# Softmax attention beside a feature-map attention on one core: part of the first score maxima computed from score differences

## The chip, the cores and the metric

The kernel runs on one core of a Trainium2 chip. The core has five engines that run at the same time, each with its own in-order queue of instructions: TensorE (PE, matrix products into PSUM), VectorE (DVE), ScalarE (ACT), GpSimd (POOL) and SyncE (SP, which here only issues DMAs). PSUM has eight banks of 128 partitions by 512 fp32 columns. The metric is the device time of one execution in microseconds (us), the median over several runs.

## The reference

Two attention layers stand side by side, and their outputs are concatenated along the features. Sequence length is 2048, model width 512, 32 heads of 16 features; inputs are bf16.

```python
# A: softmax attention
qkv = (x @ wqkv) -> q, k, v           # each [32 heads, 2048, 16]
scores = einsum("bhqd,bhkd->bhqk", q, k) * 16 ** -0.5
p = softmax(scores, axis=-1)
a = einsum("bhqk,bhkd->bhqd", p, v) -> [2048, 512] @ wo
# B: linear attention with a softmax feature map
pq, pk = q @ w_phi, k @ w_phi          # per head, 16 x 16
phi = concat([softmax(p), softmax(-p)])
kv, z = phi_k^T v, sum_s phi_k
b = (phi_q kv) / (phi_q z + 1e-6) -> [2048, 512] @ wo
out = concatenate([a, b], axis=-1)
```

Layer A has 32 x 2048 x 2048 scores, and every one of them is computed twice: once to find each row's maximum, once to take the exponential. Layer B is small and runs beside it.

## The kernel before, in words

**Tiling of layer A.** The heads are packed in 8 groups `g` of four heads, one head in each quarter of 32 partitions (`QT`, `KT`: [128, 8, 2048], queries and keys with features on partitions). Two groups share one projection: a matrix product of 128 output columns gives eight heads, of which the even four belong to one group and the odd four to the other. `proj_kq` makes one such chunk of 512 positions: four PE matmuls, then for the very first chunk ("direct") two ACT passes that mask the bank into the two groups, and for all others a staging copy by ACT into `SG` (line 553) and two POOL passes that mask it (lines 557 and 561). The keys carry ones in the unused feature rows, so that the queries can carry the negated row maximum there.

**Units.** The work is cut in units of a group and a stretch of queries: first four units of 128 queries (group 0, queries 0 to 511), then units of 256, at the end units of 128 again. Each unit passes through:

1. *Maxima* (`try_m1`, `try_m1_of`): for every 128 queries, each of the four heads (`r`, a row quarter of PE) and each of the four key chunks `kc` of 512, one matmul writes a bank of 128 queries by 512 scores (line 944). DVE reduces two banks at a time to two columns of `part` (line 952). A full unit has its columns reduced once more to the row maximum (`row_max`, line 974). For the first four units and the last ones the maximum goes into the queries by two short DVE operations (lines 985, 986), a PE transposition (line 988) and a DVE addition (line 991); for the others by POOL and two DMAs.
2. *Exponentials* (`try_m2`): the scores are computed again, transposed, with the maximum already subtracted by the extra rows (line 1034), and ACT takes `exp(0.25 s)` from a bank into a slot of the ring `pT` (28 slots).
3. *Values* (`try_pv`, line 1100): PE multiplies the slots with `VP`, the values with a column of ones, which gives the sums too; then the division, and the output projection.

**Layer B** runs in 32 steps (`fm`), the first released at 40 us and then one every 29.5 us. Its buffers `pB`, `uB` and `oB` are not used before that.

**What sets the order.** The order of all instructions is written out beforehand by a planner in the kernel's own code: a simulation with fixed durations per instruction. Each engine takes, whenever it is free, the ready instruction of the lowest `prio`; PE decides by the backlogs of DVE and ACT whether it feeds the maxima or the exponentials next, and fits in projections ("jobs", each with a due number `want`) and dummy matmuls (lines 1336 and 1351) where they do not hurt. `job_late` gives the price that a waiting job may put on the scores; before 60 us it is so high that any ready job goes ahead. Some two dozen weights of these decisions are drawn anew for every 36 us of the plan from a list of numbers, `SEEDS0`. The resulting order is fixed in the program, with semaphores between the engines.

**The start.** The first 512 rows of x come by plain loads into `SG` and are transposed by PE (`turn_x(0, t)`), the next 512 by one load into an unused slice of `QT` and by PE as well; rows 1024 to 2047 come by DMA transposes straight into `xAT` (line 496), in four pieces for each 512 rows. The weights of the first projections are loaded in two small pieces, the rest in three large ones behind the first transposes.

Of the kernel before, what the change touches and what calls it, by code (L numbers as in the profile page):

```python
# [7 lines left out]
ALU = mybir.AluOpType  # L8
# [172 lines left out]
def bass_concat_heads__softmax_full_mha__linear_kernel_hedgehog__prompt_kernel(  # L181
# [8 lines left out]
    NKT = 16  # L190
    NC = 4
    RING = 28
    SEG = 36
    SEEDS0 = [484, 2, 930, 619226, 78, 78407, 78375275, 78375663478, 78375275210, 78375275322, 78375275348780669,
              337514, 422, 709462, 422743, 709830676, 422280059592, 422280059592983, 1365, 680, 874585, 933,
              704, 134, 317297294, 227, 219559, 961, 141970821483, 219559543039, 154753, 268, 80, 80802]
    VB = 7

    BW = 18
# [8 lines left out]
    for c in range(NC):  # L208
        for g in range(NG):
# [3 lines left out]
            for q0, nq in cuts:  # L213
                units.append((g, c, 512 * c + q0, nq))
    NU = len(units)

    with contextlib.ExitStack() as es:
        block = es.enter_context(nc.Block())
# [265 lines left out]
        for t in range(4):  # L484
# [5 lines left out]
        dma("xn4", lambda e: e.dma_start(  # L490
            QT[:, 5, :].rearrange("p (t n) -> p t n", n=512),
            A_x[0][512:1024, :].rearrange("(t p) n -> p t n", p=128)), (), [("Q", 5, k) for k in range(NC)], prio=0.1,
            us=0.5, land=5.8)
        for c in range(2, NC):
            for ct in range(4):
                dma("xa%d" % c, lambda e, ct=ct, c=c: e.dma_start_transpose(
                    xAT[:, ct, c * 512:(c + 1) * 512], A_x[0][c * 512:(c + 1) * 512, ct * 128:(ct + 1) * 128]), (),
                    [("xA", c, ct)], prio=0.3 if c == 2 else 0.7, us=1.29, land=5.0)
# [24 lines left out]
        def proj_kq(kind, G, c, want, direct):  # L523
            col = (0 if kind == "q" else 512) + 128 * G
            T = QT if kind == "q" else KT
            K = "Q" if kind == "q" else "K"
            sl = slice(c * 512, (c + 1) * 512)
            j = job(quads(lambda e, b, ct: e.matmul(  # L528
                PS[:, b, :], wA[:, ct, col:col + 128], xAT[:, ct, sl], start=(ct == 0), stop=(ct == 3))),
                want, [("wA", 0 if kind == "q" else 1) + ((0,) if G == 0 else ())] + [("xA", c, t) for t in range(4)])  # L530
            projs.append(j.node)
            if kind == "k":
                kv_projs.append(j.node)
            if direct:
                n = []
                for gl in range(2):
                    g = 2 * G + gl
                    if kind == "q":
                        n.append(act(
                            lambda g=g: T[:, g, sl], lambda: PS[:, j.bank, :], ACT.Copy, 512, ["kmask"],  # L540
                            [(K, g, c)], n[:1], prio=1, scale=kmask[:, gl:gl + 1]))
                    else:
                        n.append(act(
                            lambda g=g: T[:, g, sl], lambda: PS[:, j.bank, :], ACT.Identity, 512,
                            ["kmask", "kone"], [(K, g, c)], n[:1], prio=1 + 0.5 * gl, scale=kmask[:, gl:gl + 1],
                            bias=kone[:, 1 - gl:2 - gl]))
                    kq_nodes[(kind, g, c)] = n[-1]
                    n[-1].deps.append(j.node)
                n[-1].frees = ("G", j)
                return  # L550
            k = stg[0] % 4
            stg[0] += 1
            evac(j, act(lambda: SG[:, k, :], lambda: PS[:, j.bank, :], ACT.Copy, 512, (), [("SG", k)], prio=2))
            for gl in range(2):
                g = 2 * G + gl
                if kind == "q":
                    kq_nodes[(kind, g, c)] = pool(lambda e, g=g, gl=gl: e.tensor_scalar(
                        T[:, g, sl], SG[:, k, :], kmask[:, gl:gl + 1], kmask[:, gl:gl + 1], ALU.mult, ALU.mult), 0.8,
                        [("SG", k), "kmask"], [(K, g, c)], prio=1)
                else:  # L560
                    kq_nodes[(kind, g, c)] = pool(lambda e, g=g, gl=gl: e.tensor_scalar(  # L561
                        T[:, g, sl], SG[:, k, :], kmask[:, gl:gl + 1], kone[:, 1 - gl:2 - gl], ALU.mult, ALU.add),
                        0.72, [("SG", k), "kmask", "kone"], [(K, g, c)], prio=1)
# [22 lines left out]
            return [kq_nodes[("q", g, c, a)] for a, b_ in QCUT if a < q0 + nq and b_ > q0]  # L586

        QCUT = ((0, 128), (128, 512))

        def proj_v(kt, want):  # L590
            j = job(quads(lambda e, b, ct: e.matmul(  # L591
                PS[:, b, :], xAT[:, ct, kt * 128:(kt + 1) * 128], wA[:, ct, 1024:1536],
                start=(ct == 0), stop=(ct == 3))), want, [("wA", 2)] + (
                    [("xA", kt // 4, kt % 4)] if kt < 8 else [("xA", kt // 4, ct) for ct in range(4)]))
            projs.append(j.node)
            kv_projs.append(j.node)
            v_nodes[kt] = evac(j, act(
                lambda: VP[:, kt, :, 0:16], lambda: PS[:, j.bank, :].rearrange("p (h d) -> p h d", d=16), ACT.Copy,
                512, (), [("V", kt)], prio=2))

        def turn_x(c, t):
            src = (lambda: SG[:, t, :]) if c == 0 else (lambda: QT[:, 4 + c, 512 * t:512 * t + 512])
            j = job(quads(lambda e, b, ct: e.matmul(
                PS[:, b, ct * 128:(ct + 1) * 128], src()[:, ct * 128:(ct + 1) * 128], ident[:],
                start=(ct == 0), stop=True, skip_group_check=True)), (-10 if c == 0 else 1.5) + 0.1 * t, ["ident"] + (
                    [("SG", t)] if c == 0 else [("Q", 4 + c, k) for k in range(NC)]), cols=128)
            projs.append(j.node)
            s0 = 512 * c + 128 * t
            keys = [("xA", c, t)]
            if t % 2 and c == 0:  # L610
                n = dve(lambda e: e.tensor_copy(
                    xAT[:, :, s0:s0 + 128], PS[:, j.bank, :].rearrange("p (a b) -> p a b", b=128)), 512, (), keys, prio=0)
# [8 lines left out]
        proj_kq("k", 0, 0, 0, True)  # L621
        for a, b_ in QCUT:
            first_q(a, b_, -0.5 if a == 0 else 1)
        for c in range(1, NC):
            if c == 1:
                for t in range(4):
                    turn_x(c, t)
            proj_kq("k", 0, c, 2 * c, False)
# [275 lines left out]
        def try_m1(single):  # L904
            u0 = m1["u"]
            for u in range(u0, 4 if u0 < 4 else min(u0 + 1, NU)):
                if u not in m1_of:
                    m1_of[u] = {"m": 0, "left": [], "half": None}
                if m1_of[u]["m"] < units[u][3] // 8 and try_m1_of(u, m1_of[u], single):
                    return True  # L910
            return False

        def try_m1_of(u, sm, single):
# [36 lines left out]
            off = p_off(u)  # L950
            deps = [n] + [rm_nodes[v] for v in range(u - 4, u - 1) if v in rm_nodes and v % 2 == ub]
            d = dve(lambda e: e.tensor_reduce(  # L952
                part[:, ub, off + m:off + m + k], PS[:, banks[0]:banks[-1] + 1, :],
# [6 lines left out]
            if sm["m"] == nq // 128 * 16:  # L960
# [3 lines left out]
            return True  # L964

        def p_off(u):
            return 16 * (u // 2) if u < 4 else 0
# [1 line left out]
        def row_max(u):  # L969
# [3 lines left out]
            off = p_off(u)  # L973
            rm_nodes[u] = dve(lambda e: e.tensor_reduce(  # L974
                mrow[:, ub, 0:4 * nt].rearrange("p (r q) -> p r q", r=4),
                part[:, ub, off:off + 16 * nt].rearrange(
                    "p (q k r) -> p r q k", r=4, q=nt), AX.X, ALU.max), 16 * nt + 40, (),
                [("mrow", ub)], r1_nodes[u], prio=0)
            mv = mrow[:, ub, 0:4 * nt]
# [386 lines left out]
        def try_pe():  # L1366
# [20 lines left out]
            for e in (("dve", "act") if d <= a + K.DA else ("act", "dve")):  # L1387
                if e == "dve" and d < K.TM and try_m1(d < K.DS):
                    return True
                if e == "act" and a < K.TA and slots_ready() and try_m2():  # L1390
                    return True
            if d >= K.TM:
# [258 lines left out]
```

## Time and profile before

| | |
|---|---|
| median of 3 runs | 1216.81 us (1216.23 to 1217.08) |
| the profiled execution | 1216.89 us |
| its span, first to last instruction | 1215.2 us |
| busy: PE, DVE, ACT, POOL | 1191.8, 1179.7, 1162.4, 841.5 us |
| granted TensorE clock | 1.000 |

How to read the lines that follow: L952 is line 952 of the kernel; an instruction is named by its engine, its operation and what it writes from what, for instance `part<-PS` for a reduction from PSUM into the tile `part`. Many ACT instructions carry line 398 and many DVE copies line 402 or 611, since one helper records them; they are told apart by their tiles. In a row of groups, the first number behind the bar is the time in which at least one instruction of the group ran, the second the mean length in ns of one; behind the second bar stands the idle time of the engine in front of them and what ended it. One instruction's bar is longer than its step, because the next one begins before it has drained. In a row of a timeline the first number is the start, the second the length of a run of equal instructions, and the bracket the idle time before. In the chain of waits a row is a stretch of the chain that ended last. In a table by stage the columns are: stretch, length, busy us and count of each engine, granted clock, share of DMA, GB/s.

### The profile page before, as it was taken

What the parts mean: (1) busy time and instruction counts of PE and PEld (TensorE: products, weight loads), DVE (VectorE), ACT (ScalarE), POOL (GpSimd) and SP (SyncE); (2) the same over time, 40 slices, a digit from 0 to 9 for tenths busy, and PEclk for the clock granted to TensorE, in tenths of its full rate; (3) what the DMA queues carried; (4) which work ended last, traced back from release to release, by engine and by line L of the source; (5) the groups of instructions that cost most, each with busy time, mean ns of one, the idle gap of its engine ahead of it and who ended that gap; (6) DMA issues with size and microseconds to landing.
All of it is one profiled execution on the core that took longest, in us unless ns stands there. A gap on an engine that the chain in (4) does not pass through costs nothing.

```text
span 1215.2 us, 39617 instructions
## 1 busy us (share of the span) xinstructions
PE 1191.8 (98%) x16953; PEld 574.2 (47%) x16953; DVE 1179.7 (97%) x1124; ACT 1162.4 (96%) x2364; POOL 841.5 (69%) x1194
## 2 busy tenths in 40 slices
PE   8999999999999999999999999999999999999998
PEld 4443444444444444544444444444444444545565
DVE  6999999999999999999999999999999999999993
ACT  4889999999999999999999999999999999999998
POOL 5498888776766766778898888888889894311120
PEclk9999999999999999999999999999999999999999
DMA  8200010001000100011112112111111111000000
GB/s 200 46 6 6 9 24 9 9 6 26 9 11 21 25 7 9 14 27 18 21 29 42 39 24 34 31 29 21 27 26 28 30 35 25 17 10 9 10 11 22
DMA packets 100209, 30.49 MB, mean 25 GB/s; under 512 B 87488, under 2 KB 100032, under 8 KB 100032
## 3 DMA queue, kind: packets, MB, share of 16 engines
q1 hardware_dynamic: 99072, 27.49, 11.4%
q8 instruction: 133, 2.18, 0.7%
q10 hardware_dynamic: 960, 0.46, 0.1%
q14 instruction: 44, 0.36, 0.1%
HBM read 4.21 MB, written 4.19 MB: 7 GB/s over the span
## 4 chain that ended last, share of the span: by engine, by line
ACT 37%; DVE 34%; PE 28%; DMA 0%; issue 0%; ACTq 0%; DVEq 0%
DVE part L952 34%; ACT pT L398 33%; PE PS L1034 9%; PE PS L944 5%; PE PS L1336 4%; PE PS L1100 4%; PE PS L825 1%; ACT eB L398 1%; PE PS L1351 1%; PE PS L684 1%; PE PS L591 1%; PE PS L528 1%; PE PS L761 1%; ACT X L398 1%; ACT xAT L398 1%; DMA wA<-in_A_wqkv_dram 0%
## 5 line engine op out<-in xcount | busy, mean ns | idle before, releaser
L952 DVE TENSOR_REDUCE part<-PS 128x2 f32<-128x1024 f32 x1024 | 1168.9, 1209 | 9.3 <-PE PS L944 5.2
L398 ACT ACTIVATE pT<-PS 128x512 bf16<-128x512 f32 x2034 | 1051.4, 690 | 20.5 <-PE PS L1034 11.5
L1034 PE MATMUL PS<-QT,KT 32*128 32x256 bf16 (+1 forms) x4480 | 700.2, 263 | 7.3 <-ACT pT L398 1.3
L1336 PE MATMUL PS<-zmv,ones_t 32*128 32x256 bf16 x3753 | 602.8, 271 | 0.3
L944 PE MATMUL PS<-KT,QT 32*128 32x512 bf16 x2570 | 482.2, 382 | 6.5 <-DVE part L952 4.1
L1034 PEld LDWEIGHTS PS<-QT,KT 32*128 32x128 bf16 x4480 | 242.3, 92 | 269.5 <-ACT pT L398 182.5
L1336 PEld LDWEIGHTS PS<-zmv,ones_t 32*128 32x128 bf16 x3753 | 284.7, 92 | 33.5 <-ACT X L398 3.7
L1100 PE MATMUL PS<-pT,VP 128*17 128x256 bf16 (+1 forms) x4480 | 195.6, 266 | 2.1 <-ACT pT L398 0.7
L944 PEld LDWEIGHTS PS<-KT,QT 32*128 32x128 bf16 x2570 | 124.6, 91 | 128.3 <-DVE part L952 64.5
L1161 POOL TENSOR_TENSOR lr<-lr,cons 128x8 f32<-128x8 f32 (+1 forms) x66 | 104.7, 1587 | 55.1 <-DMA lr<-X 55.1
L1100 PEld LDWEIGHTS PS<-pT,VP 128*17 128x17 bf16 x4480 | 68.5, 88 | 98.9 <-issue 83.4
L804 POOL TENSOR_TENSOR den_t<-den_t,cons 128x32 f32<-128x32 f32 x16 | 87.2, 5451 | 0.5
L711 POOL TENSOR_SCALAR sB<-sB 128x256 f32<-128x256 f32 (+2 forms) x96 | 68.8, 716 | 6.6
L747 POOL TENSOR_TENSOR wA<-eB,rB 128x1024 bf16<-128x1024 bf16 x32 | 61.7, 1927 | 14.8 <-ACT rB L398 14.6
L1171 POOL TENSOR_TENSOR QT<-X,Yd 128x256 bf16<-128x256 f32 (+1 forms) x66 | 45.7, 692 | 36.7 <-DMA Yd<-Yd 36.6
L724 POOL TENSOR_TENSOR sB<-eB 128x512 f32<-128x512 bf16 x32 | 36.9, 1153 | 45.4 <-ACT eB L398 45.4
L998 POOL TENSOR_SCALAR stage<-mrow 128x8 bf16<-128x8 f32 (+1 forms) x64 | 15.4, 240 | 75.4 <-DVE mrow L974 75.2
L709 POOL TENSOR_TENSOR sB<-uB 128x256 f32<-128x256 f32 (+2 forms) x96 | 45.7, 476 | 5.8
L698 POOL TENSOR_TENSOR sB<-pB 128x256 f32<-128x256 f32 x32 | 23.1, 721 | 32.8 <-ACT pB L398 32.3
L1351 PE MATMUL PS<-zmv,ones_t 128*32 128x512 bf16 x464 | 42.0, 386 | 0.2 <-ACT X L398 0.2
L561 POOL TENSOR_SCALAR KT<-SG,kmask,kone 128x512 bf16<-128x512 bf16 x30 | 22.7, 768 | 27.1 <-ACT SG L398 27.1
L713 POOL TENSOR_TENSOR uB<-sB,uB 128x256 f32<-128x256 f32 x64 | 37.8, 591 | 3.8
(118 smaller groups left out, 817.5 us busy)
## 6 DMA issues: line engine op xcount, KB each, us to landing
Yd<-Yd SPq DMA_DIRECT2D x232, 16.0 KB, 2.2
out_dram<-xAT SPq DMA_DIRECT2D x16, 128.0 KB, 1.7
out_dram<-OA SPq DMA_DIRECT2D x15, 128.0 KB, 1.7
QT<-mcols SPq DMA_DIRECT2D x116, 2.0 KB
mcols<-stage SPq DMA_TRANSPOSE x64, 2.3
lr<-X SPq DMA_DIRECT2D x58, 4.0 KB
Yd<-lr SPq DMA_DIRECT2D x58, 4.0 KB
wA<-in_A_wqkv_dram SPq DMA_DIRECT2D x2, 384.0 KB, 4.8
```

Of the source, the lines that this page charges most:

```text
L398: n = mk("act", lambda ds: P.op("act", lambda e: e.activation(out_(), in_(), func, **kw), ds), reads, writes, deps, occ=c + (0.093 if sbuf ...
L709: pool(lambda e, w=w, rw=rw: e.tensor_tensor(rw, t3[:, :, 0:w], t3[:, :, w:2 * w], ALU.subtract), us, tb, ["sB"])
L711: pool(lambda e, w=w: e.tensor_scalar(sB[:, 0:64 * w], sB[:, 0:64 * w], 1.0, 0.0, ALU.mult, ALU.max), us1, ["sB"], ["sB"])
L747: pool(lambda e: e.tensor_tensor(phiB[k].rearrange("p (g f) -> p g f", f=16), e3, rB[:, i, :].unsqueeze(2).broadcast_to([128, 64, 16]), AL ...
L804: pool(lambda e: e.tensor_tensor(den_t[:, :], den_t[:, :], cons[:, 0:32], ALU.pow), 5.42, ["cons"], ["den"])
L944: fns = [lambda e, rr=rows[i], b=banks[i]: e.matmul(PS[:, b, :], QT[32 * rr:32 * rr + 32, g, q0 + 128 * qt:q0 + 128 * qt + 128], KT[32 * r ...
L952: d = dve(lambda e: e.tensor_reduce(part[:, ub, off + m:off + m + k], PS[:, banks[0]:banks[-1] + 1, :], AX.X, ALU.max), 512 * k, (), (), d ...
L1034: fns = [lambda e, kt=kg * ns + j, j=j: e.matmul(PS[:, bank, j * nq:(j + 1) * nq], KT[32 * r:32 * r + 32, g, kt * 128:(kt + 1) * 128], QT[ ...
L1100: fns.append(lambda e, r=r, s=s, kt=kt, j=j: e.matmul(PS[32 * r:32 * r + 17, VB, 0:nq], VP[:, kt, 8 * (g // 2) + 2 * r + g % 2, :], pT[:, ...
L1161: pool(lambda e: e.tensor_tensor(lr[:, ub, 0:nr], lr[:, ub, 0:nr], cons[:, 0:nr], ALU.pow), 0.17 * nr + 0.2, ["cons"], [("lr", ub)], prio=2)
L1336: n = pe_op([lambda e, r=r: e.matmul(PS[:, VB, 0:FW], ones_t[32 * r:32 * r + 32, :], zmv[32 * r:32 * r + 32, 0:FW], tile_position=(32 * r, ...
L1351: pe_op([lambda e, q=q: e.matmul(PS[32 * q:32 * q + 32, VB, :], ones_t[:, 0:32], zmv[:, :], tile_position=(0, 32 * q), **kw) for q in rang ...
```

## The change

Four things change.

1. *Maxima from differences.* For the first four units (group 0, 128 queries each), `DIFF` marks pairs of key chunks: the pair of chunks 2 and 3 in all four units and the pair of chunks 0 and 1 in units 2 and 3, which is six groups of four heads, 24 pairs of banks. For such a pair, PE computes the difference of the two banks (queries times chunk kc+1, plus the negated queries in `oB` times chunk kc, into one bank), ACT takes its ReLU into one of four fp32 buffers (`uB` and `pB` of layer B), PE computes the bank of chunk kc, and one DVE instruction adds the two and reduces the sum with a maximum: max(a, b) = a + relu(b - a). A group of pairs may begin only before 36 us (`DT`); one that has not begun then goes the old way. POOL makes the negated queries.
2. *x rows 1024 to 1535* are loaded plainly into a slice of `QT` and transposed by PE (`turn_x(2, t)`), as rows 512 to 1023 were already. The DMA transposes of the last 512 rows get the rank of the earlier ones.
3. *First K projection*, chunks 1 to 3: the even group's half is masked by ACT straight from PSUM (`direct == 2`), the odd half goes through `SG` and POOL as before.
4. *The planner*: the high price of a late job holds until 18 us (`JT`) and not until 60 us, the due numbers of two chunks move, and all the numbers in `SEEDS0` are others.

```diff
+    DT = 36
+    KM = 2
+    JT = 18
...
+    DIFF = "01,01,11,11".split(",")
...
-        dma("xn4", lambda e: e.dma_start(
...
-        for c in range(2, NC):
+        for c in (1, 2):
+            dma("xn%d" % (4 * c), lambda e, c=c: e.dma_start(
+                QT[:, 4 + c, :].rearrange("p (t n) -> p t n", n=512),
+                A_x[0][512 * c:512 * c + 512, :].rearrange("(t p) n -> p t n", p=128)), (),
+                [("Q", 4 + c, k) for k in range(NC)], prio=0.1, us=0.5, land=5.8)
+        for c in range(3, NC):
             for ct in range(4):
                 dma("xa%d" % c, lambda e, ct=ct, c=c: e.dma_start_transpose(
...
-                for gl in range(2):
+                for gl in range(1 if direct == 2 else 2):
...
+        def neg_q():
+            for a, b_ in QCUT:
+                qn_nodes[a] = pool(lambda e, a=a, b_=b_: e.tensor_scalar(
+                    oB[:, a:b_], QT[:, 0, a:b_], -1.0, 1.0, ALU.mult, ALU.mult), 0.3 if a == 0 else 0.65, (), ["oB"],
+                    [kq_nodes[("q", 0, 0, a)]], prio=0)
...
+        RD = [(uB[:, 0:512], ("uB", 0)), (uB[:, 512:1024], ("uB", 1)), (pB[:, 0, :], ("pB", 0)),
+              (pB[:, 1, :], ("pB", 1))]
...
+        def try_diff():
...
+                fns = [lambda e, a=a, i=i: e.matmul(
+                    PS[:, b, :], a[32 * r:32 * r + 32, q0:q0 + 128],
+                    KT[32 * r:32 * r + 32, g, (kc + i) * 512:(kc + i + 1) * 512],
+                    start=(i == 1), stop=(i == 0), tile_position=(32 * r, 0)) for a, i in ((QT[:, g, :], 1), (oB, 0))]
+                n = pe_op(fns, need, "row", (r, r), (b,))
+                k = rd_free.pop(0)
+                buf, key = RD[k]
+                x = act(lambda: buf, lambda: PS[:, b, :], ACT.Relu, 512, (), [key], [n], prio=0.5)
...
+        def try_sum(u, sm):
...
+                n = pe_op(fns, [x], "row", (r,), (b,))
...
+                d = dve(lambda e: e.tensor_tensor_reduce(
+                    buf, PS[:, b, :], buf, 1.0, -3.0e38, ALU.add, ALU.max, part[:, u % 2, o:o + 1]), 530, (), [key],
+                    [n, x], prio=1)
...
+                if e == "act" and a < K.TA and m1["u"] < len(DIFF) and try_diff():
+                    return True
...
         def job_late(now):
-            if now < 60.0:
+            if now < JT:
                 return 9.0
```

More of the change, by code (lines that the diff above doesn't have):

```diff
@@ L907, in try_m1 @@
                 if u not in m1_of:
-                    m1_of[u] = {"m": 0, "left": [], "half": None}
-                if m1_of[u]["m"] < units[u][3] // 8 and try_m1_of(u, m1_of[u], single):
-                    return True
+                    m1_of[u] = {"m": 0, "left": [], "half": None, "p": 0, "dl": None, "al": []}
+                sm = m1_of[u]
+                if sm["m"] < units[u][3] // 8:
+                    if by_diff(u, sm["m"]):
+                        if try_sum(u, sm):
+                            return True
+                    elif try_m1_of(u, sm, single):
+                        return True
@@ new lines, in try_sum @@
+        def try_sum(u, sm):
+            now = state["now"]
+            g, c, q0, nq = units[u]
+            kc = sm["m"] // 4 % 4
+            if nfree() < 1 or held["m"] >= 4:
+                return False
+            for ent in sm["al"]:
+                r, k, x = ent
+                if x.start is None or not pe_ok("row", (r,)):
+                    continue
+                if x.done > now + 0.4:
+                    push(x.done - 0.4)
+                    continue
+                sm["al"].remove(ent)
+                b = take("m", 1)[0]
+                fns = [lambda e: e.matmul(
+                    PS[:, b, :], QT[32 * r:32 * r + 32, g, q0:q0 + 128],
+                    KT[32 * r:32 * r + 32, g, kc * 512:(kc + 1) * 512],
+                    start=True, stop=True, tile_position=(32 * r, 0))]
+                n = pe_op(fns, [x], "row", (r,), (b,))
+                buf, key = RD[k]
+                o = p_off(u) + sm["p"] + r
+                d = dve(lambda e: e.tensor_tensor_reduce(
+                    buf, PS[:, b, :], buf, 1.0, -3.0e38, ALU.add, ALU.max, part[:, u % 2, o:o + 1]), 530, (), [key],
+                    [n, x], prio=1)
+                d.frees = [("m", b)]
+                rd_free.append(k)
+                r1_nodes.setdefault(u, []).append(d)
+                last["m1"] = (fns, (r,), n, d)
+                if not sm["dl"] and not sm["al"]:
+                    sm["m"] += 8
+                    sm["p"] += 4
+                    sm["dl"] = None
+                    group_done(u, sm)
+                return True
@@ L975, in row_max @@
                 mrow[:, ub, 0:4 * nt].rearrange("p (r q) -> p r q", r=4),
-                part[:, ub, off:off + 16 * nt].rearrange(
+                part[:, ub, off:off + m1_of[u]["p"]].rearrange(
                     "p (q k r) -> p r q k", r=4, q=nt), AX.X, ALU.max), 16 * nt + 40, (),
```

77 lines of the change are left out of this document (59 added, 18 removed).

## The prediction

> **What bounds the kernel now.** I read the page's busy shares and slices first, then a table by stage, then the chain of waits, then the timelines of the first 60 us.
>
> ```profile
> span 1215.2 us, 39617 instructions
> PE 1191.8 (98%) x16953; PEld 574.2 (47%) x16953; DVE 1179.7 (97%) x1124; ACT 1162.4 (96%) x2364; POOL 841.5 (69%) x1194
> ...
> ACT 37%; DVE 34%; PE 28%; DMA 0%; issue 0%; ACTq 0%; DVEq 0%
> ```
>
> Three engines look full. PE's share is padded, because lines 1336 and 1351 are dummy matmuls; VectorE (DVE) and ScalarE (ACT) share the chain almost evenly. So it must be seen, stage by stage, which of the two has room:
>
> ```profile
> core 0: us, PE busy (x) PEld busy (x) DVE busy (x) ACT busy (x) POOL busy (x), PEclk, DMA share, GB/s
> 11.00:35.00 24.00, 23.03 (x166) 9.84 (x167) 20.35 (x21) 14.15 (x26) 8.10 (x13) 1.00 0.77 184
> 35.00:60.00 25.00, 24.10 (x282) 11.71 (x280) 24.89 (x33) 20.94 (x41) 10.74 (x15) 1.00 0.17 39
> 60.00:100.00 40.00, 37.81 (x552) 18.27 (x551) 39.64 (x38) 35.55 (x73) 36.65 (x57) 1.00 0.04 6
> 100.00:1100.00 1000.00, 989.00 (x13683) 463.30 (x13681) 997.74 (x928) 981.91 (x2008) 757.48 (x1043) 1.00 0.11 21
> 1100.00:1192.20 92.20, 91.12 (x1762) 54.22 (x1759) 91.44 (x93) 86.58 (x181) 18.81 (x39) 1.00 0.06 10
> 1192.20:1215.30 23.10, 18.40 (x458) 10.47 (x454) 3.63 (x11) 19.42 (x37) 0.00 (x0) 1.00 0.08 26
> ```
>
> DVE is idle for 2.26 + 0.76 = 3.0 us between 100 and 1192 us: from 100 us until its last score maximum (1192.2 us) it alone sets the pace. ACT is idle for 9.85 us in 11 to 35, 4.06 in 35 to 60 and 4.45 in 60 to 100: 18.4 us in all, for it waits there for the first maxima. From 100 to 1192 ACT shows 18.1 + 5.6 = 23.7 us of idle time in small pieces. After 1192.2 us ACT works off the exponentials that are left, and the run ends 23 us later:
>
> ```profile
> core 0: us, PE busy (x) PEld busy (x) ACT busy (x), PEclk, DMA share, GB/s
> ...
> 110.00:1180.00 1070.00, 182.20 (x3968) 61.25 (x3968) 982.57 (x1910) 1.00 0.11 21
> ...
> 1192.20:1216.00 23.80, 5.11 (x292) 4.04 (x288) 17.47 (x28) 1.00 0.08 25
> ```
>
> These are the instructions that touch the exponentials' tile pT: 28 ACT instructions, 17.5 us, come after the last maximum. So two clocks run one behind the other, DVE's and ACT's, and the end is ACT's. A gain on DVE is worth its full size only if ACT is earlier too.
>
> **The change, part by part.** The prices:
>
> ```profile
> L952 DVE TENSOR_REDUCE part<-PS 128x2 f32<-128x1024 f32 x1024 | 1168.9, 1209 | 9.3 <-PE PS L944 5.2 <-PE PS L1034 2.3 <-PE PS L1336 0.2
> L991 DVE TENSOR_TENSOR QT<-PS,QT 128x128 bf16<-128x128 f32 x6 | 1.7, 279 | 0.0
> L611 DVE CAST xAT<-PS 128x512 bf16<-128x512 f32 x2 | 1.3, 684 | 5.3 <-PE PS L603 5.3
> L402 DVE COPY X<-PS 128x128 f32<-128x128 f32 x2 | 0.6, 290 | 5.0 <-PE PS L1113 5.0
> ```
>
> ```profile
> 44.97 0.09 DVE mrow L974
> ...
> 93.08 18.10 DVE part L952 x16
> ...
> 590.66 10.78 ACT pT L398 x22
> ```
>
> *24 pairs.* Two banks cost one reduction; back to back that is 18.10/16 = 1.131 us. Now ACT takes ReLU(S1-S0) of one bank and DVE adds S0 and takes the maximum over one bank. The trace has no such instruction. From below: one pass over 512 columns cannot be under half of 1.131, 0.57. From above: if the second operand doubled the time, 1.13, nothing saved. Nearest rows: the two 512-column CASTs out of PSUM take 1.3 us together, each 0.684, so the second starts about 0.61 after the first; and a TENSOR_TENSOR with two inputs (279 ns for 128 columns) is no dearer than a COPY with one (290). I take 0.61. DVE saves 24 x (1.131 - 0.61) = 12.5 us, between 0 and 24 x 0.56 = 13.5. The Trainium skill, "VectorE: DVE Perf Modes", § Two Vector instructions with no wait between them, says that an op which also writes out its accumulator is two instructions, the main one and an accumulator read. No instruction of this trace writes an accumulator, so the trace cannot judge it. At the step of the shortest DVE row above (0.09) that would take 24 x 0.09 = 2.2 us off the saving, 10.3 in place of 12.5; I leave it out of the sum and keep it in the range.
>
> ACT pays 24 ReLUs over 128x512 from PSUM; its exponentials of that shape step at 10.78/22 = 0.49 us: 24 x 0.49 = 11.8 us.
>
> *The rest on ACT:*
>
> ```profile
> 12.23 0.81 ACT L398 ACTIVATE KT<-PS,kone,kmask 128x512 bf16<-128x512 f32 x1
> 12.26 0.40 PE L603 MATMUL PS<-ident,QT 128*128 128x128 bf16 x4
> 12.90 0.63 ACT L398 ACTIVATE xAT<-PS 128x512 bf16<-128x512 f32 x1
> ...
> 19.88 0.60 ACT L398 ACTIVATE VP<-PS 128x512 bf16<-128x512 f32 x1 [4.32 <-PE PS L591]
> ```
>
> Turning rows 1024 to 1535 on PE adds four jobs of four 128-column matmuls (0.40 us each, 1.6 in all, where PE runs dummies) and four ACT copies: 4 x 0.49 = 2.0 us. The even half of K, chunks 1 to 3, is a scaled and biased ACT pass straight from PSUM (0.67 us from its start at 12.23 to the next at 12.90): 3 x 0.67 = 2.0 us; the staging copy stays, for the odd half. ACT's added work is 11.8 + 2.0 + 2.0 = 15.8 us, against 18.4 us of idle time before 100 us. It fits, but little is left. If that cover were gone, all 15.8 us would be on ACT's clock.
>
> *Off the path:*
>
> ```profile
> 14.81 3.03 POOL L561 TENSOR_SCALAR KT<-SG,kmask,kone 128x512 bf16<-128x512 bf16 x4 [4.42 <-ACT SG L398]
> ...
> 2.73 5.54 SPq L496 DMA_TRANSPOSE xAT<-in_A_x_dram  x4
> ...
> 10.04 5.20 SPq L496 DMA_TRANSPOSE xAT<-in_A_x_dram  x4
> ...
> 1.73 5.67 DMA wA<-in_A_wqkv_dram
> ```
>
> POOL loses three K passes of 0.76 us and gains the negated Q (512 columns in two pieces, some 0.8 us by the same row); it works 8.1 of the 24 us, so that is free. SP issues one 512 KB load in place of four transposes (5.54 us); the transposes of the last chunk move from 10.04 to about 3.3, ahead of the big weight loads, which move from 8.3 (2.73 + 5.54) to some 8.8, and what stands behind them (Wo, the other branch's weights) goes out about 5 us sooner. The new load shares the DMA engines with the first K weights, which land at 7.40 (1.73 + 5.67) and start everything: at the 184 GB/s of the table's first row 512 KB are 2.8 us of transfer; with half of that in the way of the weights the start is 1.4 us later, and since 512 KB of transposes leave the same place, it may as well be 1.4 us sooner; I take 0, in the middle.
>
> *PE's jobs (JT 60 to 18) and DVE's waits:*
>
> ```profile
> 11.02 3.71 DVE L952 TENSOR_REDUCE part<-PS 128x2 f32<-128x1024 f32 x3 [2.41 <-PE PS L944]
> 15.29 4.79 DVE L952 TENSOR_REDUCE part<-PS 128x2 f32<-128x1024 f32 x4 [0.56 <-PE PS L944]
> 21.01 3.48 DVE L952 TENSOR_REDUCE part<-PS 128x2 f32<-128x1024 f32 x3 [0.94 <-PE PS L944]
> 25.32 3.49 DVE L952 TENSOR_REDUCE part<-PS 128x2 f32<-128x1024 f32 x3 [0.83 <-PE PS L944]
> ...
> 29.64 1.23 DVE L952 TENSOR_REDUCE part<-PS 128x2 f32<-128x1024 f32 x1 [0.32 <-PE PS L944]
> ...
> 34.03 2.36 DVE L952 TENSOR_REDUCE part<-PS 128x2 f32<-128x1024 f32 x2 [0.71 <-PE PS L1034]
> ...
> 27.44 1.83 PE PS L591 x8
> ```
>
> Behind its first reduction DVE waits 0.56 + 0.94 + 0.83 + 0.32 + 0.71 = 3.4 us, mostly for score matmuls that stand behind pairs of V projections (1.83 us, line 591, in the chain). From 18 us on such jobs now yield, and chunk 3 of x comes earlier: up to 3.4 us back. But the change adds a wait: DVE's in-order sum needs a ReLU, which needs a score difference, and behind a waiting sum stand the row maxima that release the exponentials. ACT must give DVE a ReLU (0.49) per 0.61 us while it also copies K, V and x. I take 0.5 us of the 3.4 as net gain, range -6 to +3.4.
>
> *New draws.* All 34 planner draws change, so the order of everything changes. DVE has 3.0 us to win in 100 to 1192, with no such bound on a loss; I take 0, range -4 to +3.
>
> **The sum.** DVE's clock: 12.5 + 0.5 = 13.0 us earlier at the last maximum. ACT's clock: 18.4 - 15.8 = 2.6 us earlier at 100 us if DVE's lead lets it run without gaps. The gap of 10.4 us must come from ACT's 23.7 us of small gaps in 100 to 1192 and from the tail, where no maxima compete. Nothing in the trace says how much of them DVE's larger lead can fill; I take half, 5.2: 2.6 + 5.2 = 7.8 us. Span 1215.2 - 7.8 = 1207.4. The profiled execution took 1216.89, 1.7 us more than its span: 1209.1. That execution is 0.1 us from the median of 1216.81, so I say 1209.
>
> **Rivals.**
> *ACT follows fully.* If all the small gaps can be used, the end moves with DVE: 1216.8 - 13 = 1204, and with all 3.4 us of the waits back 1201. For it: ACT is more idle than DVE in every stage. Against: a single exponential shows a longer bar than its step, so ACT's true room is uncertain, and gaps behind PE's job bursts do not go away with a larger lead.
> *ACT is the clock.* If the small gaps are PE's, only the head's 2.6 us remain: 1214.2; and if some of the six groups begin after 36 us, where the code goes back to plain reductions, each gives up 4 x 0.52 = 2.1 us of DVE's saving, so that little of the change takes place: 1214 to 1218. Against: ACT has 9.85 us idle in the very stretch where the groups run.
> *Slower: ReLUs arrive late.* Place: 15 to 45 us. DVE's price per pair is then not 0.61 but ACT's spacing of the ReLUs. One copy (0.49) between two ReLUs makes 0.98; at 1.13 the saving is gone; with two copies it is 1.47, and 24 x (1.47 - 1.13) = 8.1 us are lost while ACT's head is no earlier: 1225. It decides from 1.23 us per pair on (2.4 us lost). For it: 16 V, 4 x and several K copies fall into that stretch. Against: the ReLUs have a better rank (0.5) than V and staging copies (2). The same comes about if the sum itself runs at half rate: at 1.13 nothing is saved on DVE, the DVE clock loses its waits, and 1217 to 1220 follows. [...]
>
> **Chances.** About 0.2% (2.4 us) is what a measurement of this kernel can tell from no change. Forecast (1205 to 1213) 0.48; ACT follows fully 0.21; ACT the clock, or few groups run 0.14, nearly all within 0.2%; late ReLUs or a dear sum 0.17, slower. So faster 0.69, same 0.14, slower 0.17. The range is 1201 to 1219: it leaves out the slower case and a sliver below the fastest. The forecast's own range is 1205 to 1213.
>
> **What would show it.** The new DVE group: 24 instructions with a step near 0.61 (right) or 1.1 (half rate). The 24 ReLUs on ACT between 15 and 40 us. The last maximum near 1179 instead of 1192.2, and a longer tail behind it, 25 to 29 us instead of 23. ACT's idle time in 11 to 100 us under 6 instead of 18.4. DVE's waits behind the first reduction at 3 us or less. It is wrong if DVE idles before the sums for ACT, if the K weights land after 8.5 us, or if DVE's idle time in 100 to 1192 grows past 5 us.

## The result and the profile after

The changed kernel takes 1211.16 us (median of 6 runs, 1210.99 to 1212.92) against 1216.53 us before (6 runs, 1216.18 to 1217.08). The ratio is 0.996, 95% interval 0.9947 to 0.9972: 5.4 us faster, by medians. The profiled execution has a span of 1209.4 us, 5.8 less than before. The page's shares and chain come first:

```profile
span 1209.4 us, 39536 instructions
PE 1186.3 (98%) x16833; PEld 569.1 (47%) x16833; DVE 1173.3 (97%) x1195; ACT 1174.2 (97%) x2393; POOL 838.9 (69%) x1193
...
ACT 48%; PE 28%; DVE 22%; POOL 1%; issue 1%; DMA 0%; ACTq 0%; DVEq 0%; POOLq 0%
```

DVE's and ACT's busy times, 17 us apart before, are now 1 us apart, and of the chain that ended last ACT has 48% in place of 37, DVE 22% in place of 34. The table by stage has the cuts of the one before, except that the last maximum is now at 1187.0 us:

```profile
core 0: us, PE busy (x) PEld busy (x) DVE busy (x) ACT busy (x) POOL busy (x), PEclk, DMA share, GB/s
11.00:35.00 24.00, 22.46 (x159) 7.67 (x157) 22.69 (x57) 22.64 (x44) 8.07 (x16) 1.00 0.94 174
35.00:60.00 25.00, 24.29 (x272) 11.55 (x273) 24.43 (x35) 21.45 (x40) 3.82 (x8) 1.00 0.18 33
60.00:100.00 40.00, 39.46 (x574) 19.75 (x573) 39.52 (x39) 36.80 (x74) 28.49 (x46) 1.00 0.06 11
100.00:1100.00 1000.00, 987.30 (x13614) 462.58 (x13609) 995.52 (x965) 988.23 (x2024) 773.37 (x1065) 1.00 0.11 21
1100.00:1187.00 87.00, 85.79 (x1718) 50.45 (x1714) 86.24 (x90) 82.49 (x173) 17.37 (x35) 1.00 0.06 10
1187.00:1209.50 22.50, 18.72 (x444) 10.80 (x442) 2.95 (x10) 18.76 (x38) 0.00 (x0) 1.00 0.08 27
```

Both clocks can be read from this table and the one before, by adding the busy columns and taking the rest of each stage as idle.

**DVE, 11 us to the last maximum.** Busy 1174.1 before, 1168.4 now: 5.7 less. Idle 7.1 before, 7.6 now. Together 5.2 us, and the last maximum moved by 1192.2 - 1187.0 = 5.2.

**ACT, 11 us to the end.** Busy 1158.6 before, 1170.4 now: 11.8 more. Idle 45.8 before, 28.1 now: 17.6 less. Together 5.8 us, the change of the span. The idle time came from before 100 us (18.4 to 8.1) and from 100 us to the last maximum (23.7 to 16.3); behind that it is 3.7 in both.

The new instructions, and DVE's reductions, by groups (the numbers behind the bar are busy time and the mean length of one, and behind the second bar the idle time ahead):

```profile
L1058 DVE TENSOR_REDUCE part<-PS 128x2 f32<-128x1024 f32 x957 | 1095.4, 1213 | 7.6 <-PE PS L1050 3.8 <-PE PS L1144 1.2 <-PE PS L1446 0.9
L1058 DVE TENSOR_REDUCE part<-PS 128x1 f32<-128x512 f32 x86 | 54.4, 681 | 1.7 <-PE PS L1144 1.0 <-PE PS L1446 0.2
...
L1004 DVE CUSTOM_DVE_ANT_0 uB<-PS,uB 128x512 f32<-128x512 f32 x12 | 8.2, 686 | 0.1
L1004 DVE CUSTOM_DVE_ANT_0 pB<-PS,pB 128x512 f32<-128x512 f32 x12 | 8.2, 685 | 0.4 <-PE PS L997 0.2
L1004 DVE DVE_READ_ACCUMULATOR2_ANT part<- 128x1 f32 x24 | 2.0, 82 | 0.0
...
L406 DVE COPY pB<-PS 128x512 f32<-128x512 f32 x2 | 1.4, 686 | 0.0
...
L406 DVE COPY X<-PS 128x256 f32<-128x256 f32 x2 | 0.8, 420 | 0.0
...
L406 DVE CAST vB<-PS 128x512 bf16<-128x512 f32 x1 | 0.7, 683 | 0.0
```

All 24 pairs took the new way, and DVE waited 0.1 + 0.4 = 0.5 us in all ahead of the sums. The timeline gives the step of a sum:

```profile
10.99 3.71 DVE L1058 TENSOR_REDUCE part<-PS 128x2 f32<-128x1024 f32 x3 [2.41 <-PE PS L1050]
15.40 6.01 DVE L1058 TENSOR_REDUCE part<-PS 128x2 f32<-128x1024 f32 x5 [0.70 <-PE PS L1050]
21.33 0.68 DVE L1004 CUSTOM_DVE_ANT_0 uB<-PS,uB 128x512 f32<-128x512 f32 x1
21.94 0.08 DVE L1004 DVE_READ_ACCUMULATOR2_ANT part<- 128x1 f32 x1
21.94 0.69 DVE L1004 CUSTOM_DVE_ANT_0 pB<-PS,pB 128x512 f32<-128x512 f32 x1
22.55 0.08 DVE L1004 DVE_READ_ACCUMULATOR2_ANT part<- 128x1 f32 x1
```

From 21.33 to 21.94 to 22.55: 0.61 us for each sum. It is shown as two instructions, but where the next instruction is ready it starts at the same moment as the accumulator read (both at 21.94), so the pair costs no more than the sum.

How far ACT is ahead can be counted in the table by stage of the instructions on the exponentials' tile, first of the kernel before, then of the changed one:

```profile
core 0: us, PE busy (x) PEld busy (x) ACT busy (x), PEclk, DMA share, GB/s
0.00:110.00 110.00, 7.66 (x288) 4.01 (x288) 46.76 (x85) 1.00 0.31 71
110.00:1010.00 900.00, 150.25 (x3168) 49.55 (x3168) 819.86 (x1587) 1.00 0.11 22
1010.00:1160.00 150.00, 27.88 (x640) 9.37 (x640) 142.71 (x286) 1.00 0.07 14
```

```profile
core 0: us, PE busy (x) PEld busy (x) ACT busy (x), PEclk, DMA share, GB/s
0.00:110.00 110.00, 7.52 (x296) 4.42 (x296) 48.67 (x88) 1.00 0.36 71
110.00:1010.00 900.00, 149.77 (x3184) 49.82 (x3184) 825.45 (x1593) 1.00 0.11 22
1010.00:1160.00 150.00, 27.55 (x664) 9.98 (x664) 143.73 (x288) 1.00 0.07 14
```

At 110 us the changed kernel is 3 exponentials ahead, at 1010 us 3 + 6 = 9, at 1160 us 11. At 0.49 us each that is 1.5, 4.4 and 5.4 us: only a quarter of the gain exists when the changed part of the program is over, and the rest is collected from ACT's small gaps in the 1000 us that follow.

### The profile page after: what moved, and what is told of

Same layout as the page of the kernel before. It is cut to its first block, busy times and chain, and to the rows that moved or that the text cites. A ratio compares the mean times of both kernels' runs of the same rounds, so it can differ in the third digit from the quotient of the medians.

```text
span 1209.4 us, 39536 instructions
## 1 busy us (share of the span) xinstructions
PE 1186.3 (98%) x16833; PEld 569.1 (47%) x16833; DVE 1173.3 (97%) x1195; ACT 1174.2 (97%) x2393; POOL 838.9 (69%) x1193
## 3 DMA queue, kind: packets, MB, share of 16 engines
HBM read 4.73 MB, written 4.19 MB: 7 GB/s over the span
## 4 chain that ended last, share of the span: by engine, by line
ACT 48%; PE 28%; DVE 22%; POOL 1%; issue 1%; DMA 0%; ACTq 0%; DVEq 0%; POOLq 0%
ACT pT L402 42%; DVE part L1058 21%; PE PS L1144 8%; PE PS L1050 5%; PE PS L1446 4%; PE PS L1210 3%; PE PS L533 2%; ACT eB L402 2%; PE PS L701 1%; ACT pB L402 1%; PE PS L607 1%; PE PS L1461 1%; ACT xAT L402 1%; ACT X L402 1%; PE PS L778 1%
## 5 line engine op out<-in xcount | busy, mean ns | idle before, releaser
L1058 DVE TENSOR_REDUCE part<-PS 128x2 f32<-128x1024 f32 (+1 forms) x1043 | 1146.6, 1169 | 9.3 <-PE PS L1050 3.8
L1446 PE MATMUL PS<-zmv,ones_t 32*128 32x256 bf16 x3638 | 583.2, 271 | 1.1 <-ACT pB L402 0.7
L1446 PEld LDWEIGHTS PS<-zmv,ones_t 32*128 32x128 bf16 x3638 | 275.3, 92 | 36.0 <-ACT X L402 3.6
L741 POOL TENSOR_TENSOR sB<-eB 128x512 f32<-128x512 bf16 x32 | 36.9, 1152 | 58.6 <-ACT eB L402 58.6
L1281 POOL TENSOR_TENSOR QT<-X,Yd 128x256 bf16<-128x256 f32 (+1 forms) x66 | 45.8, 693 | 35.4 <-DMA Yd<-Yd 35.4
L744 POOL TENSOR_TENSOR sB<-sB 128x256 f32<-128x256 f32 x64 | 36.1, 563 | 3.1
L1461 PE MATMUL PS<-zmv,ones_t 128*32 128x512 bf16 x408 | 36.9, 386 | 0.0
```

What stands on the lines that cost most here:

```text
L1058: d = dve(lambda e: e.tensor_reduce(part[:, ub, off + m:off + m + k], PS[:, banks[0]:banks[-1] + 1, :], AX.X, ALU.max), 512 * k, (), (), d ...
L1281: mul_nodes[u] = pool(lambda e, a=a: e.tensor_tensor(QT[:, g, q0 + a:q0 + a + w], X[:, ub, a:a + w], Yd[:, ub, a:a + w], ALU.mult), w * 0. ...
L1446: n = pe_op([lambda e, r=r: e.matmul(PS[:, VB, 0:FW], ones_t[32 * r:32 * r + 32, :], zmv[32 * r:32 * r + 32, 0:FW], tile_position=(32 * r, ...
L1461: pe_op([lambda e, q=q: e.matmul(PS[32 * q:32 * q + 32, VB, :], ones_t[:, 0:32], zmv[:, :], tile_position=(0, 32 * q), **kw) for q in rang ...
```

## The experiments

Two questions were open. Why does a saving of 12.5 us on DVE become 5 to 6: because ACT follows and only about half can reach the end (theory C, two clocks), or because the change is worth the whole saving and its new list `SEEDS0` is less favourable than the old one (theory D, the draws)? And what holds the rest?

**First try: both kernels without a list.** `SEEDS0 = [0]` gives every draw its middle value. The first kernel is the one before, the second the changed one, the third the changed one without the pairs.

```diff
-    SEEDS0 = [...]
+    SEEDS0 = [0]
```

```diff
-    DIFF = "01,01,11,11".split(",")
+    DIFF = "00,00,00,00".split(",")
...
-        neg_q()
```

> The kernel before with the planner's middle values in every segment in place of its list of 34 draws (SEEDS0 = [0]), to be compared with e2, which has the same for the changed kernel. Theory D (the draws): the change itself is worth what DVE saves, and the new list is less favourable than the old one; then e1 is slower than the kernel before by 10 us or more, and e1 minus e2 is 10 to 14 us. Theory C (two clocks): only about half of DVE's 12.5 us can reach the end because ScalarE follows; then e1 minus e2 is 4 to 8 us, as with the lists.

> The changed kernel with the planner's middle values in every segment. Theory D: 10 to 14 us below e1, and DVE takes fewer single-bank reductions in 100 to 1192 us than the 86 of the changed kernel's profile. Theory C: 4 to 8 us below e1.

> As e2, but no pair is computed from differences and the negated queries are not made: x rows 1024 to 1535 turned by PE, half of the first K on ScalarE and the earlier end of the high job price remain. By my sum these three are worth at most 3.4 us of DVE's waits and cost ScalarE 4 us: within 4 us of e1, either way; and e3 minus e2 is what the pairs alone are worth: about 12 us under theory D, 4 to 8 us under theory C.

Measured: 1247.07 (ratio 1.0238, 1.0194 to 1.0282), 1228.62 (1.0106, 1.0068 to 1.0145) and 1252.32 us (1.028, 1.0238 to 1.0321). Differences of 18 and 24 us are more than any theory had. The slices of the first of the three show why they can't be used: the TensorE clock was granted in full in every slice of the two original kernels, but not here.

```profile
PEclk9999999999999999996999998989999979999999
```

The mean clock was 0.973, 0.990 and 0.971. The order of the three times is the order of their clocks, so a slower TensorE is mixed with the effect that was looked for. Inconclusive.

**Second: a saving on DVE alone, in a fixed order.** The order of the kernel before is kept, and some of its reductions read fewer columns, so that DVE loses about the 12.5 us that the pairs take from it, and ACT gets nothing to do. Once at the head (the first four units), once in the middle (units 20 and 21), where ACT has no idle stretch.

```diff
+            cw = 325 if u < 4 else 512
...
-                part[:, ub, off + m:off + m + k], PS[:, banks[0]:banks[-1] + 1, :],
+                part[:, ub, off + m:off + m + k], PS[:, banks[0]:banks[-1] + 1, 0:cw],
```

> The kernel before, its order of instructions untouched; only the 32 score reductions of the first four units read 2 x 325 of their 2 x 512 columns (a part of the scores is left out of their maxima), which takes 32 x 374 / 960 = 12.5 us from DVE in the head and adds nothing to ScalarE. It measures what DVE's saving alone is worth when nothing is planned anew. If DVE is the clock: 11 to 12.5 us faster. Two clocks with half passing on: about 6. If ScalarE is the clock: 0 to 3.

> The same shortening (32 reductions, 12.5 us of DVE) in units 20 and 21, in the middle of the run, order untouched. DVE the clock: 11 to 12.5 us faster; half: about 6; ScalarE the clock: 0 to 3. A large difference from e4 would mean that the head has a limit of its own.

Measured: 1215.20 us against 1216.71 (ratio 0.9991, 0.9982 to 1.0001), and with `20 <= u < 22` in place of `u < 4` 1218.12 us (1.0007, 0.9997 to 1.0016). Next to nothing of the 12.5 us arrives, and neither difference is clear of the noise. The first one's groups and table by stage:

```profile
L953 DVE TENSOR_REDUCE part<-PS 128x2 f32<-128x650 f32 x32 | 25.9, 831 | 15.2 <-PE PS L944 9.6 <-PE PS L1035 4.0 <-PE PS L1337 1.7
```

```profile
11.00:35.00 24.00, 23.88 (x174) 10.15 (x176) 14.54 (x23) 14.26 (x27) 9.05 (x14) 1.00 0.99 177
35.00:60.00 25.00, 24.36 (x295) 12.21 (x290) 20.27 (x32) 21.75 (x43) 11.47 (x15) 1.00 0.17 39
```

DVE is idle for 9.46 + 4.73 = 14.2 us of these 49, against 3.65 + 0.11 = 3.8 before: 10.4 of the 12.5 us have become waits for score matmuls. Where the order of instructions stays, DVE can't run ahead; a lead needs an order that has been planned for it.

**Third: the same saving on ACT, and on both.** The exponentials of units 20 and 21 are shortened by about the same (64 times a bar of 0.60 less one of 0.407 is 12.4 us), alone and together with the reductions; the last run of this kind shortens those exponentials that stand beside the short reductions in the order.

```diff
+            ce = 278 if 20 <= u < 22 else 512
...
-            ex = act(lambda: pT[:, slot, :], lambda: PS[:, bank, :], ACT.Exp, 512, (), (), deps, prio=4, scale=0.25)
+            ex = act(lambda: pT[:, slot, 0:ce], lambda: PS[:, bank, 0:ce], ACT.Exp, 512, (), (), deps, prio=4, scale=0.25)
```

> The kernel before, order untouched; the 64 exponentials of units 20 and 21 write 278 of their 512 columns (the rest of those probabilities is left as it was), which takes 64 x 234 / 1200 = 12.5 us from ScalarE. If DVE is the clock: 0 to 2 us faster. Two clocks: 4 to 6. ScalarE the clock: 11 to 12.5.

> The kernel before with its own list and its order untouched; in units 20 and 21 both the 32 reductions are shortened as in e5 and the 64 exponentials as in e6 (parts of scores and probabilities left out), 12.5 us from each engine. e5 and e6, one engine each, moved the end by about nothing. If the two engines hold each other in lockstep through TensorE's fixed order, both together give 9 to 12.5 us. If TensorE's own stream is the third limit there, 0 to 4.

Measured: ACT alone 1216.89 us (1.0000, 0.9991 to 1.001), both 1216.22 us (1.0000, 0.9991 to 1.0009). The second has a flaw that its table by stage shows:

```profile
340.00:390.00 50.00, 48.42 (x627) 20.88 (x631) 39.95 (x48) 48.60 (x99) 35.22 (x53) 1.00 0.08 19
390.00:440.00 50.00, 47.06 (x687) 22.95 (x689) 50.00 (x48) 39.16 (x104) 37.89 (x56) 1.00 0.12 18
```

DVE has room (39.95 of 50 us) while ACT is full, and ACT has room only 50 us later, when DVE is full: a unit's exponentials follow its maxima by a unit. So it was done again with `20 <= m1["u"] < 22`, the exponentials that are computed while those maxima are.

> In e7 the two shortened stretches lay one behind the other: DVE works on units 20 and 21 at 348 to 388 us, ScalarE on the same units at 390 to 432 us, and in each stretch the other engine stayed full. Here the order is again that of the kernel before, the 32 reductions of units 20 and 21 are shortened as in e5, and the exponentials that are planned beside them (some 66 of other units) write 278 of 512 columns, so that both engines lose about 12.5 us of work in the same 40 us (parts of scores and probabilities are left out). If DVE and ScalarE hold each other: 8 to 12 us faster. If TensorE's stream, dummies among it, is as long as the stretch: 0 to 4 us.

Measured: 1213.04 us against 1216.91 (0.9968, 0.9959 to 0.9978): 3.9 us faster. Of these runs, only the one with both engines relieved at the same place brings a clear saving to the end, and then a third of it. The groups of the stretch 330 to 400 us:

```profile
L953 DVE TENSOR_REDUCE part<-PS 128x2 f32<-128x650 f32 x32 | 26.2, 834 | 6.5 <-PE PS L1338 3.3 <-PE PS L1035 2.4 <-PE PS L944 0.4
...
L398 ACT ACTIVATE pT<-PS 128x278 bf16<-128x278 f32 x61 | 21.6, 407 | 7.4 <-PE PS L944 2.6 <-PE PS L1035 2.5 <-PE PS L1338 2.1
```

Both engines now wait in front of these instructions, and only for PE: for score matmuls (lines 944 and 1035) and for dummies (line 1338).

**Fourth: are the dummies the rest?** As the last one, with the dummies of that stretch cut to a quarter of their columns.

```diff
+                        fw = 64 if 20 <= m1["u"] < 22 else FW
...
+                cf = 128 if 20 <= m1["u"] < 22 else 512
```

> As e8 (both engines lose 12.5 us of work in the same 40 us, order untouched; parts of scores and probabilities are left out), and the dummy matmuls that are planned in that stretch are cut to a quarter of their columns. In e8 the end moved by 3.9 us and both engines then waited for TensorE, 6.5 and 7.4 us. If it is the dummies' time in TensorE's stream that holds them: 9 to 12 us faster than before. If it is TensorE's real work and its turns between the engines: 4 to 6 us, as e8. If the TensorE clock drops in that stretch, slower than e8.

Measured: 1211.58 us against 1217.03 (0.9957, 0.9941 to 0.9974), at a clock of 1.0. That is 5.45 us, 1.6 more than with full dummies (all four executions lie below the ten of the run before). DVE's waits in that stretch fall only from 6.5 to 5.3 us:

```profile
L953 DVE TENSOR_REDUCE part<-PS 128x2 f32<-128x650 f32 x32 | 25.9, 831 | 5.3 <-PE PS L1035 2.4 <-PE PS L1339 1.4 <-PE PS L944 1.2
```

The cut took only part of the dummies' time away: by the profiles of the two runs, dummies keep PE busy for 18.7 us between 340 and 390 us, against 23.5 before the cut. So dummies hold at least 1.6 of the 12.5 us. The 7 that are left lie in what remains of the dummies, in PE's real matmuls or in the turns in which the three engines hand banks to each other; these were not told apart.

**Fifth: the change with equal lists.** Theory C against theory D again, this time with lists that one and the same short search chose for each of the three kernels, under a limit that keeps PE evenly loaded.

```diff
-    SEEDS0 = [...]
+    SEEDS0 = [477, 999, 999653, 999504, ...]
```

The changed kernel has `[84, 0, 105, 740, ...]`; the third has `[988, 988945, 966, 161, ...]`, `DIFF = "00,00,00,00"` and no `neg_q()`.

> The kernel before with a list of draws that comes from a short search over the planner's own planned end (segment by segment, 40 draws each, plans whose matmul work sinks too low in any 3.4 us left out so that the TensorE clock stays at 1.000). f2 and f3 have lists from the same search, so none of the three has a list that was fitted longer. Expected: granted clock 1.000; slower than the kernel before with its own list by some 8 to 14 us. Theory D (draws): f1 minus f2 is 8 to 14 us, more than the 5.4 us between the two lists as they are. Theory C (two clocks): 4 to 8 us.

> The changed kernel with a list from the same short search. Theory D: 8 to 14 us faster than f1, and some 8 us slower than the changed kernel with its own list. Theory C: 4 to 8 us faster than f1.

> The changed kernel without the 24 pairs (plain reductions for all first banks, no negated queries), list from the same short search. Between f1 and f2: the pairs alone (f3 minus f2) 5 to 9 us, the other three parts (f1 minus f3) 1 to 5 us. If the prediction's terms hold (net waits 0.5 us, ScalarE's 4 us of extra work hidden), f1 minus f3 is near 0.5 us and all the rest is the pairs'.

Measured, against 1216.87 us: before 1226.24 (1.0088, 1.0069 to 1.0106), changed 1220.35 (1.003, 1.0019 to 1.0041), changed without the pairs 1224.16 (1.0058, 1.0042 to 1.0075). The mean clock was 1.0, 0.999 and 0.998. The second and third ran one stretch of the start at a lower clock; this is the stage 5 to 15 us of the second (of the third, 0.83 as well; of the first, 1.00):

```profile
5.00:15.00 10.00, 7.02 (x49) 3.58 (x47) 4.07 (x6) 4.42 (x10) 5.74 (x12) 0.83 1.06 265
```

0.17 of 10 us is 1.7 us of PE's time; against the first kernel the differences can only be larger for that. The executions whose mean clock was 1.000 took 1226.0, 1220.0 and 1222.9 us (medians of three, four and two).

With equal lists the change is worth 1226.24 - 1220.35 = 5.9 us (6.0 among the executions with a clock of 1.000), nearly the 5.4 us of the two originals: inside theory C's 4 to 8, below theory D's 8 to 14. The list of the kernel before is worth 1226.24 - 1216.87 = 9.4 us over the short search's, that of the changed kernel 1220.35 - 1211.16 = 9.2: no sign that either suits its kernel better. The other sign named for theory D, fewer single-bank reductions than the changed kernel's 86, goes both ways: 24 with the middle values, 112 here. Of the 5.9 us the pairs bring 1224.16 - 1220.35 = 3.8 (2.9 at that clock), less than the 5 to 9 expected; the other three parts together bring 1226.24 - 1224.16 = 2.1 (3.1), more than the 0.5 that the prediction's terms would give. Each kernel had one list only, so how much such a difference scatters from list to list was not measured: theory D is made unlikely by this, not excluded, and the split between the pairs and the rest is rough.

The count of exponentials looks different in this pair: at 110 us the changed kernel has done 76 against 95, at 1160 us 1952 against 1940. How much of the gain shows early depends on what the list puts first; that most of it is collected late holds in both pairs.

## Why the prediction was right, and where it was not

The forecast was 1209, its own range 1205 to 1213; 1211.16 was measured, and the gain was 5.4 to 5.8 us in place of 7.8.

- **The sum's price, "I take 0.61": right.** 0.61 us per pair, so DVE saved 24 x (1.131 - 0.61) = 12.5 us. The Trainium skill, "VectorE: DVE Perf Modes", § Two Vector instructions with no wait between them, is borne out in that an accumulator read of 82 ns follows each sum, but the 2.2 us that this could have cost do not appear in the step of sums that stand back to back. The half rate that the prediction kept as a rival (1.13 us) did not come about for this pair of sources, PSUM and SBUF.
- **Late ReLUs: refuted.** ACT's 24 ReLUs ran from 17.5 to 36.9 us, and the sums waited 0.5 us. From the first start (17.51) to the last (36.28) they stand 0.82 us apart on average, under the 1.23 us from which the spacing would have decided; five single gaps are longer, up to 2.0 us, but DVE had plain reductions, short operations and finished ReLUs to go on with.
- **The start, "I take 0": right.** The first reduction begins at 10.99 us (11.02 before), although the transposes of the last x rows take 6.79 us to issue, against the 5.54 of the four that went out first before.
- **DVE's waits, "0.5 us of the 3.4": too low.** DVE is idle for 1.3 us from 11 to 35 us, against 3.65: 2.3 us won.
- **DVE "13.0 us earlier at the last maximum": wrong.** It was 5.2. The step that failed is that the sum carried the head's lead to the end in full: it read DVE as the engine that "alone sets the pace" from 100 us on, and for *New draws* it said "I take 0, range -4 to +3". At the head the lead was there: by the timelines, first of before, then of the changed kernel, the row maxima of the fourth unit are done 15.0 us sooner,

```profile
54.71 0.16 DVE L974 TENSOR_REDUCE mrow<-part 128x4 f32<-128x16 f32 x1
```

```profile
39.67 0.15 DVE L1084 TENSOR_REDUCE mrow<-part 128x4 f32<-128x8 f32 x1
```

close to the 12.5 + 2.3 = 14.8 of the two points above. Then the new order spends it. 86 reductions take one bank where before all took two: at 0.60 each (the bar of 0.681 less the 0.08 by which bars of two banks exceed their step of 1.131) 51.6 us, against 43 x 1.131 = 48.6: 3.0 lost. Three full and two half copies out of PSUM, less one that went back to ACT, are done by DVE: 1.9. From 35 us to the last maximum DVE is idle for 6.3 us, against 3.5: 2.8. Of the 9.6 us between 14.8 and 5.2 that leaves 1.9 unresolved. The two kernels with equal lists lose as much; first the one before, then the changed one:

```profile
56.00 0.17 DVE L972 TENSOR_REDUCE mrow<-part 128x4 f32<-128x16 f32 x1
...
1197.18 2.94 DVE L950 TENSOR_REDUCE part<-PS 128x1 f32<-128x512 f32 x3
```

```profile
40.42 0.16 DVE L1082 TENSOR_REDUCE mrow<-part 128x4 f32<-128x8 f32 x1
...
1190.42 3.48 DVE L1056 TENSOR_REDUCE part<-PS 128x2 f32<-128x1024 f32 x3
```

The row maxima of the fourth unit are done 15.6 us sooner, the last maximum (1200.1 and 1193.9) only 6.2: 9.4 us are lost, although there the reductions of one bank grow only from 76 to 112. So the loss does not belong to one list alone. It fits the runs in a fixed order, where 12.5 us off DVE alone came to next to nothing, that DVE can't leave the other engines behind; how an order made for the lead spends it was not tested by itself. In the original pair, DVE's idle time from 100 us on grew to 5.2, just past the 5 that the prediction named as a sign against it.
- **ACT's clock: the mechanism right, three sizes off.** The added work shows as 11.8 us and not 15.8; the copies that DVE took over account for about 1.7 of the difference (3 x 0.49 and 2 x 0.38, less the one that came back), and the rest probably lies between bars and steps (a bar ahead of a gap counts 0.60, its step 0.49, and there are fewer gaps). ACT's idle time before 100 us was to be filled; 8.1 us stayed, against "under 6". The gaps behind 100 us gave 23.7 - 16.3 = 7.4, more than "half, 5.2". Counted in exponentials, the head gave 1.5 us in place of 2.6, the rest 3.9 in place of 5.2.
- **"A longer tail, 25 to 29 us": wrong.** It is 22.5 us. With the lead spent, DVE finishes no farther ahead of ACT than before (with equal lists 1.1 us farther, 25.2 against 24.1).
- **The rivals.** *ACT follows fully* needed DVE's 13 us at the end, which the order gave back. *ACT is the clock* would have needed groups that begin too late, or no gain behind the head; all 24 pairs ran, and 8 of the 11 exponentials were won behind it.
- **"A gain on DVE is worth its full size only if ACT is earlier too": shown**, and it was not strict enough. In a fixed order 12.5 us off DVE gave 1.5 and -1.4 (neither clear of the noise), off ACT 0, off both at the same place 3.9. PE, which the prediction set aside as padded with dummies, is a third limit: the other two then waited for it, and shorter dummies there added 1.6.

So the total came out near because the forecast had already cut DVE's saving down to what ACT could follow: the lead did not last to the end, but ACT had used enough of it by then. That it came within 2 us is in part luck. The half taken of the small gaps was a guess, as the prediction says, and ACT's three terms miss by more than the total does: 4.0 us less work was added, 8.1 us of the idle time before 100 us stayed unused, and the gaps behind gave 2.2 us more (4.0 - 8.1 + 2.2 = -1.9).

What stays open: which of the 9.6 us of lost lead the planner could have kept, since another order may trade them for waits elsewhere.

## What to carry to other kernels

Where several engines are full and hand buffers to each other in a fixed order, price a saving by what the other engines can do with it at the same place: here 12.5 us on one of them were worth next to nothing alone, and 3.9 with as much room on the second at the same place. Add up busy and idle time of each engine from the stages' table, before and after; the two sums together give the whole change, and show whether a lead was used or spent later. When the order and the draws behind it change with the idea, give both kernels lists of equal effort before the difference is called the idea's.

## What the runs showed of the hardware beyond that

- DVE adds a PSUM and an SBUF operand in fp32 and takes the maximum at the pace of one operand: 0.61 us for 512 columns, no more than the two CASTs of the kernel before, and its accumulator read (82 ns) lies beside the next instruction.
- ACT's scaled and biased pass over 512 columns of PSUM steps at 0.66 us against 0.49 for a ReLU or an exponential, as the timeline of the changed kernel shows:

```profile
16.85 0.89 ACT L402 ACTIVATE KT<-PS,kone,kmask 128x512 bf16<-128x512 f32 x1
17.51 1.20 ACT L402 ACTIVATE uB<-PS 128x512 f32<-128x512 f32 x2
18.47 0.73 ACT L402 ACTIVATE SG<-PS 128x512 bf16<-128x512 f32 x1
...
36.28 0.63 ACT L402 ACTIVATE pB<-PS 128x512 f32<-128x512 f32 x1
```

Here 17.51 - 16.85 = 0.66 for the pass, and (18.47 - 17.51)/2 = 0.48 for a ReLU, the first of which stands in the second row and the last in the last.
- The granted TensorE clock depends on the order of instructions: the same real work, its dummies placed otherwise, ran at 1.000 with one list and at 0.97 to 0.99 with the middle values. By what the clock is granted was not isolated.
